# An expert layer's first slot list moved ahead of weight conversions, and output writes that no longer wait for one another

## The chip, the cores and the metric

The kernel runs on one core of a Trainium2 chip. The metric is the device time of one execution in microseconds (us), given as the median over runs. An execution is also recorded by the hardware profiler; the recording's span is a little shorter than the execution's own time.

## The reference, cut to what matters

Four batches of 576 tokens pass through attention (8 heads, window of 128), then through a block that adds the real part of a two-dimensional Fourier transform and an MLP (512 to 2048 to 512), and then through the layer that the change touches: each token goes to one of 8 experts, which it takes from its own logits or from the token before it.

```python
for b in range(B):
    prev_e = -1
    for s in range(S):
        fresh_e = int(np.argmax(logits[b, s]))
        if s == 0 or local_gate[b, s] < 0.5:
            e = fresh_e
        else:
            e = prev_e if prev_e >= 0 else fresh_e
        prev_e = e
        ...
        h = np.maximum(x[b, s] @ w1[e], 0.0)
        out[b, s] = p[e] * (h @ w2[e])
```

x is 2304 x 512, w1[e] is 512 x 1024, w2[e] is 1024 x 512, all float32. An expert works on the tokens that chose it, and each token's row of `out` is written once.

## The kernel before

Each float32 product is made of three TensorE products (`mm3`, L171 to L173: high by high, high by low, low by high). `split` makes the two halves: the high half is a copy on ScalarE (L167, "CAST" in the trace), the low half a subtraction on VectorE (L168, which reads the high half), so every conversion of a piece of weights is one instruction on ACT and then one on DVE.

The experts are ranked by their load. The work after the MLP runs in this order. Expert "-1" is the first ranked expert's first 256 tokens (`early`); then comes r = 0, the same expert with 224 more rows and with the same weights, then r = 1 (384 rows), and so on to r = 7 (216 rows). Each is one pass of `ffn`. It runs over eight blocks of 128 hidden columns, and for each of them PE makes the hidden product `hps` (12 matmuls), ACT the relu `h` or `hE` (L631) and DVE its low half (L634). The second product `acc` of a block stands on PE behind the hidden product of the block after it. It needs the relu for its L171 and the low half for its L173.

Around `ffn` stand two generators that are taken a step at a time.

- `expert_weights(r, e)` loads four chunks c0 to c3 of an expert's weights. Each chunk is a pair of 512 KB loads on SP's queue (L1235 for w1, L1236 for w2) into one of two buffers, and four conversions, two for w1 and two for w2. The next load into a buffer waits until the four conversions that read it are done. In the trace the loads are `we<-in_w`, the converted weights `t`.
- `expert_inputs(r)` loads the slot lists of a rank (`ids`, three loads on SP), adds them on DVE (L1275), turns them into row numbers and scales `idn` (L1277, L1278), gathers the rows of x (`xg`, an indirect DMA that POOL issues, L1250, one for each 128 rows), transposes them on PE (L603, `tps`) and splits them to `xTe`.

`emit` scales a finished `acc` into `yo` on ACT (L1261, or L1257 for a folded tail) and writes it by an indirect DMA that POOL issues (L1262, `out<-yo,idn`). `yo` has two buffers. All writes go to the one tensor `out`, and each waits until the write before it has landed.

While expert -1 runs, the kernel steps through r = 1's weights and r = 0's rows (loop at L1376). Before the change `pre_.step(2)` places two conversions behind each half block, and `beside.step(TE)` takes three steps of `expert_inputs(0)`: list and first gather, second gather, first transposes. A scheduler then puts the recorded instructions into one list for each engine. The engines run their lists in order, so an instruction that waits holds up all that stands behind it on its engine. `issue_after(x)` makes the scheduler place what is recorded inside it behind x, and `behind()` is an `issue_after` on the last hidden product, relu and low half.

Of the kernel before, what the change touches and what calls it, by code (L numbers as in the profile page):

```python
# [26 lines left out]
NT = B * S  # L27
# [132 lines left out]
def build(ctx, tc, a, out):  # L160
# [5 lines left out]
    def split(hi, lo, src, eng=None):  # L166
        nc.scalar.copy(hi, src)  # L167
        return (eng or nc.vector).tensor_tensor(out=lo, in0=src, in1=hi.bitcast(F32), op=ALU.subtract)  # L168
# [445 lines left out]
    def ffn(xT, n, chunks, ps_h, acc, hidden, sums, tail=0):  # L614
# [6 lines left out]
        for f in range(nf + 1):  # L621
# [16 lines left out]
            if f > 0:  # L638
# [3 lines left out]
                for t, c in enumerate(range(0, n, P)):  # L642
                    if g == 0:
                        acc.append(sums[t % len(sums)].tile([P, DM], F32, tag=("acc0", "acc1", "acc2", "g")[t], name="acc"))
                    m = min(P, n - c)
                    if tail and m < P:
                        for j in range(2):
                            nc.tensor.matmul(acc[t][0:step + m], lhsT=h[:, c:c + step + m], rhs=t2[:, j, g % per], start=g == 0 and j == 0, stop=g == nf - 1 and j == 1)  # L648
                        continue
                    mm3(acc[t][0:m], h[:, c:c + m], h[:, low + c:low + c + m], t2[:, 0, g % per], t2[:, 1, g % per], g == 0, g == nf - 1)  # L650
                yield
# [552 lines left out]

    def expert_weights(r, e):

# [6 lines left out]
        if r < 0:  # L1213
# [3 lines left out]
            for i in range(len(loads) + RB - 1):  # L1217
# [9 lines left out]
                for m in (slice(0, n // 2), slice(n // 2, n)):  # L1227
                    split(w[:, 0, m], w[:, 1, m], x[:, m])
                    yield
            return  # L1230
        for c in range(F // CB):
            t1, t2 = chunksE[r][c]
            x = act.tile([P, 2, 4 * CB], F32, tag="xT", name="we")
            x1, x2 = x[:, 0].rearrange("p (k f) -> p k f", k=4), x[:, 1].rearrange("p (k f) -> p k f", k=per)
            nc.sync.dma_start(out=x1.unsqueeze(1), in_=w1[:, bass.ds(e, 1), :, c * CB:(c + 1) * CB])  # L1235
            nc.sync.dma_start(out=x2.unsqueeze(1), in_=w2[:, bass.ds(e, 1), c * per:(c + 1) * per, :])  # L1236
            for i in range(2):
                m = slice(2 * i, 2 * i + 2)
                split(t1[:, 0, m], t1[:, 1, m], x1[:, m])
                yield  # L1240
            for i in range(per):
                split(t2[:, 0, i], t2[:, 1, i], x2[:, i])
                yield
# [8 lines left out]

    def emit(acc, idx, m=P, both=False):
        y = act.tile([P, DM], F32, tag="y", name="yo")
# [5 lines left out]
        else:  # L1260
            nc.scalar.activation(y[0:m], acc[0:m], AF.Copy, scale=idx[0:m, 2:3].bitcast(F32))  # L1261
        nc.gpsimd.indirect_dma_start(out=out, out_offset=IOA(ap=idx[0:m, 1:2], axis=0), in_=y[0:m], in_offset=None,  # L1262
                                     bounds_check=NT - 1, oob_is_err=False)

# [6 lines left out]
    def slot_ids(x, nt, lists):  # L1271
# [5 lines left out]
        nc.vector.tensor_copy(n[:, 0:nt, 0:2], x0[:, :, 0:2])  # L1277
        nc.vector.tensor_copy(n[:, 0:nt, 2:3].bitcast(F32), x0[:, :, 2:3])  # L1278
        return n
# [96 lines left out]
    for n, _ in enumerate(ffn(xTs.pop(-1), EARLY, chunksE[-1], ps_h, acc, hidden, (ps_a, ps_a))):  # L1376
        if xp is None:
            beside.step(2 if n < 4 else 1)
        if xp is None and not beside.q:
            c2.close()  # L1380
            xp = ctx.enter_context(pool("xp", 2, reuse_waits="tile"))
            pre_.add(expert_weights(1, er[1]))
            pre_.step()
            beside.add(expert_inputs(0))
            beside.step(TE)
        elif xp is not None and n < 15:
            pre_.step(2)
    for t, x in enumerate(acc):
        emit(x, ids[-1][:, t])
    beside.drain()  # L1390

# [5 lines left out]
    def single(xT, chunks, idx):  # L1397

        acc = ps_a.tile([P, DM], F32, tag="acc0", name="acc")
        for c in range(0, len(chunks), 2):  # L1400
# [9 lines left out]
            for f in range(4):  # L1410
                t2 = chunks[c + f // per][1]
                mm3(acc, t[:, 0, f, 0:P], t[:, 1, f, 0:P], t2[:, 0, f % per], t2[:, 1, f % per], c + f == 0, c == 2 and f == 3)
        emit(acc, idx)

# [6 lines left out]
    for r in range(E):  # L1421
# [6 lines left out]
        for n, _ in enumerate(ffn(xTs.pop(r), CAPS[r], chunksE[r], ps_h, acc, hiddenE, (ps_a, ps_a, ps_a2, ps_g), tail_of(CAPS[r]))):  # L1428
            pre_.step(1 if r else 2)
            if n >= 2:  # L1430
# [65 lines left out]
```

## Time and profile before

| what | us |
|---|---|
| three runs | 969.30, 969.94, 970.32 (median 969.94) |
| the profiled execution's own time | 969.35 |
| its span in the trace | 967.6 |
| PE busy in the span | 909.6 (94%) |
| DVE / ACT / POOL busy | 513.5 / 379.7 / 241.1 |

The mean granted clock of TensorE over the span is 0.974 of full speed. An engine's busy time counts its instructions from start to end. Rows of the timeline give start, duration, engine, line, operation, result<-sources, and in brackets the idle time of the engine just before with what released it. "SPq" is the queue on which SP issues loads. A row of waits names who waited for whom, the total in us, how many times and the longest. A row of a stretch gives its bounds and length and the busy us (instructions) of PE, PEld, DVE, ACT and POOL, then the granted clock as a share of full speed, the DMA engines' busy share and GB/s.

Expert -1 ends and r = 0 begins between 705 and 725 us of the span. r = 0's products run from 724.5 to 749.9, and the last product ends near 951.

### The profile page before, as it was taken

How to read it: one execution, taken by the hardware profiler on the slowest of the kernel's cores; microseconds unless marked ns; L12 is line 12 of the kernel's file. 1: busy time of each engine (PE TensorE's matmuls, PEld its weight loads, DVE VectorE, ACT ScalarE, POOL GpSimd, SP SyncE). 2: the span in 40 equal slices, each digit the busy share in tenths (PEclk: the TensorE clock that was granted, in tenths of full speed). 3: DMA queues.
4: the chain of work that ended last, by engine and by line, in shares of the span. 5: the costliest groups of instructions: out<-in, count | busy, mean ns of one | idle time of the engine just before them, and what ended most of it. 6: DMA issues, size and time to landing. Idle time of an engine off the chain costs nothing. (4 is left out here: it accounts for less than half of the span.)

```text
span 967.6 us, 16131 instructions
## 1 busy us (share of the span) xinstructions
PE 909.6 (94%) x5889; PEld 751.8 (78%) x5889; DVE 513.5 (53%) x1308; ACT 379.7 (39%) x993; POOL 241.1 (25%) x365
## 2 busy tenths in 40 slices
PE   8988899989999999999999999998979999999993
PEld 4546576776787898899888888887758898888782
DVE  5778756835655467511334435358656446556410
ACT  4674564543553245421111111114245455445310
POOL 2314631330322046210111312123123211122100
PEclk9989999999999999999999999999989999999997
DMA  9913351541312594263554443426167555465100
GB/s 326 368 70 114 132 153 44 159 131 44 117 38 78 168 339 120 66 152 66 110 109 109 109 104 63 102 71 202 52 207 251 171 173 188 160 190 175 66 20 20
DMA packets 109037, 129.15 MB, mean 133 GB/s; under 512 B 16222, under 2 KB 78046, under 8 KB 108884
## 3 DMA queue, kind: packets, MB, share of 16 engines
q1 hardware_dynamic: 83636, 103.95, 33.4%
q0 software_dynamic: 22720, 19.36, 9.4%
q10 hardware_dynamic: 2592, 4.72, 1.3%
q8 instruction: 48, 0.79, 0.4%
q14 instruction: 41, 0.34, 0.1%
HBM read 99.65 MB, written 30.87 MB: 135 GB/s over the span
## 5 line engine op out<-in xcount | busy, mean ns | idle before, releaser
L631 ACT ACTIVATE h<-hps 128x256 fp32r<-128x256 f32 x152 | 58.2, 383 | 270.5 <-PE hps L173 267.2
L634 DVE SCALAR_TENSOR_TENSOR h<-hps,h 128x256 fp32r<-128x256 f32 x152 | 63.7, 419 | 170.0 <-ACT h L631 169.9
L171 PE MATMUL acc<-t,h 128*128 128x512 f32 x304 | 126.9, 417 | 2.1 <-ACT h L631 1.1
L173 PE MATMUL acc<-t,h 128*128 128x512 f32 x304 | 122.2, 402 | 2.2 <-DVE h L634 2.2
L172 PE MATMUL acc<-t,h 128*128 128x512 f32 x304 | 121.8, 401 | 0.3 <-POOL t L168 0.3
L168 DVE TENSOR_TENSOR t<-we,t 128x512 fp32r<-128x512 f32 x128 | 85.7, 705 | 43.2 <-ACT t L167 40.8
L167 ACT CAST t<-we 128x512 fp32r<-128x512 f32 x128 | 73.5, 619 | 38.6 <-PE acc L648 17.4
L171 PE MATMUL hps<-xT,t 128*128 128x256 f32 x288 | 85.5, 297 | 2.5 <-ACT t L167 2.2
L171 PE MATMUL hps<-xTe,t 128*128 128x320 f32 (+7 forms) x288 | 86.3, 300 | 1.1 <-ACT xTe L167 1.1
L173 PE MATMUL hps<-xT,t 128*128 128x256 f32 x288 | 83.1, 289 | 4.2 <-POOL t L168 4.2
L172 PE MATMUL hps<-xTe,t 128*128 128x320 f32 (+7 forms) x288 | 85.8, 298 | 0.0
L173 PE MATMUL hps<-xTe,t 128*128 128x320 f32 (+7 forms) x288 | 85.5, 297 | 0.0
L171 PE MATMUL hps<-xTb,t 128*128 128x256 f32 x288 | 83.2, 289 | 0.0
L172 PE MATMUL hps<-xT,t 128*128 128x256 f32 x288 | 83.1, 289 | 0.0
L172 PE MATMUL hps<-xTb,t 128*128 128x256 f32 x288 | 81.8, 284 | 0.0
L173 PE MATMUL hps<-xTb,t 128*128 128x256 f32 x288 | 81.8, 284 | 0.0
L406 ACT ACTIVATE t<-t,mx 128x128 f32<-128x128 f32 (+1 forms) x160 | 62.5, 393 | 30.5 <-DVE mx L399 26.4
L173 PEld LDWEIGHTS acc<-t,h 128*128 128x128 f32 x304 | 58.2, 192 | 17.3 <-DVE h L634 3.7
L171 PEld LDWEIGHTS acc<-t,h 128*128 128x128 f32 x304 | 57.7, 190 | 15.5 <-issue 4.4
L171 PEld LDWEIGHTS hps<-xT,t 128*128 128x128 f32 x288 | 56.4, 196 | 11.0 <-ACT t L167 3.3
L172 PEld LDWEIGHTS acc<-t,h 128*128 128x128 f32 x304 | 58.1, 191 | 7.9 <-POOL t L168 0.6
L634 DVE SCALAR_TENSOR_TENSOR hE<-hps,hE 128x256 fp32r<-128x256 f32 (+4 forms) x96 | 30.8, 349 | 61.4 <-ACT hE L631 60.4
(285 smaller groups left out, 2027.9 us busy)
## 6 DMA issues: line engine op xcount, KB each, us to landing
we<-in_w SPq DMA_DIRECT2D x64, 512.0 KB
rw<-in_w_ch SPq DMA_DIRECT2D x32, 512.0 KB
qkt<-in_qk SPq DMA_DIRECT2D x15, 642.0 KB
nd<-xT SPq DMA_DIRECT2D x18, 512.0 KB
xTb<-nd POOLq DMA_DIRECT2D x18, 512.0 KB
vt<-in_v SPq DMA_DIRECT2D x16, 384.0 KB
pd<-y ACTq DMA_DIRECT2D x18, 256.0 KB
ub<-ud SPq DMA_DIRECT2D x18, 256.0 KB
```

The source lines that it names most:

```text
L167: nc.scalar.copy(hi, src)
L168: return (eng or nc.vector).tensor_tensor(out=lo, in0=src, in1=hi.bitcast(F32), op=ALU.subtract)
L171: nc.tensor.matmul(o, lhsT=wh, rhs=xh, start=start, stop=False, **kw)
L172: nc.tensor.matmul(o, lhsT=wh, rhs=xl, start=False, stop=False, **kw)
L173: return nc.tensor.matmul(o, lhsT=wl, rhs=xh, start=False, stop=stop, **kw)
L406: nc.scalar.activation(t[0:m, j], t[0:m, j], AF.Exp, bias=mx[0:m, j:j + 1], scale=-1.0, accum_out=sums[0:m, j:j + 1])
L631: last["relu"] = nc.scalar.activation(h[:, 0:n], hps[:, 0:n], AF.Relu)
L634: last["rest"] = nc.vector.scalar_tensor_tensor(out=h[:, lo:lo + c1 - c0], in0=hps[:, c0:c1], scalar=0.0, in1=h[:, c0:c1].bitcast(F32), op ...
```

## The change

Three things change. First, r = 1's DVE conversions of weights are recorded under `issue_after(lists[0])`, where `lists[0]` is the last instruction on r = 0's list (`idn`), and the conversions of expert -1's loop are recorded under `behind()` and spread otherwise: two steps at first, then none until n is over 12. What is left of r = 1's weights (two chunks) is converted in r = 0's pass, one step for each half block and under `behind()`. Second, r = 0's first transposes are recorded behind the acc product that is last at n = 14, and the two writes of expert -1 are recorded behind the last `split`. Third, each write of `out` is declared independent of the write just before it.

```diff
@@ expert_weights
+    def expert_weights(r, e, lists=None):
+        def turn_():
+            return tc.issue_after(lists[0]) if lists else nullcontext()
+
...
+            if lists is not None and c == 0:
+                yield
             for i in range(2):
                 m = slice(2 * i, 2 * i + 2)
-                split(t1[:, 0, m], t1[:, 1, m], x1[:, m])
+                with turn_():
+                    split(t1[:, 0, m], t1[:, 1, m], x1[:, m])
                 yield
...
@@ emit
+        if alone and wrote:
+            tc.declare_no_dep(w.ins, wrote[-1], reason="each token has one slot, so the rows are others")
+        wrote.append(w.ins)
...
@@ loop of expert -1
-            pre_.add(expert_weights(1, er[1]))
+            lists = []
+            soon_ = 2
+            pre_.add(expert_weights(1, er[1], lists))
             pre_.step()
             beside.add(expert_inputs(0))
-            beside.step(TE)
+            beside.step(TM)
+            lists.append(last["idn"].ins)
         elif xp is not None and n < 15:
-            pre_.step(2)
+            with behind():
+                pre_.step(2 if soon_ or n > 12 else 0)
+            soon_ = max(soon_ - 1, 0)
+            if n == 14:
+                with tc.issue_after(last["acc"].ins):
+                    beside.step()
+    beside.drain()
     for t, x in enumerate(acc):
-        emit(x, ids[-1][:, t])
-    beside.drain()
+        with tc.issue_after(last["hi"].ins):
+            emit(x, ids[-1][:, t])
...
@@ loop over r
-            pre_.step(1 if r else 2)
+            with nullcontext() if r else behind():
+                pre_.step()
```

`last["hi"]`, `last["acc"]` and `last["idn"]` are set in `split`, `ffn` and `slot_ids`. Since each write still depends on the write two before it, at most two are under way.

On DVE near the end of expert -1, before: 7716 to 7718 are r = 1's converted weights (c0's w1, c0's w2, c1's w1), 7729 is r = 0's list, 7735 its row numbers, and h_7806 and h_7839 are hidden blocks 5 and 6.

```order
L634 SCALAR_TENSOR_TENSOR h_7806<-hps_7793,h_7806 128x256
L168 TENSOR_TENSOR t1_7716<-we_7724,t1_7716 128x512 x2
L168 TENSOR_TENSOR t2_7717<-we_7724,t2_7717 128x512
L1275 TENSOR_TENSOR ids_7729<-ids_7729 128x8
L168 TENSOR_TENSOR t2_7717<-we_7724,t2_7717 128x512
L1275 TENSOR_TENSOR ids_7729<-ids_7729 128x8
L634 SCALAR_TENSOR_TENSOR h_7839<-hps_7826,h_7839 128x256
L1277 CAST idn_7735<-ids_7729 128x2x2
L1278 COPY idn_7735<-ids_7729 128x2
L168 TENSOR_TENSOR t1_7718<-we_7778,t1_7718 128x512 x2
```

The same place after; the list is 7727, its row numbers 7733, blocks 5 to 7 are h_7790, h_7812 and h_7834.

```order
L634 SCALAR_TENSOR_TENSOR h_7790<-hps_7777,h_7790 128x256
L1287 TENSOR_TENSOR ids_7727<-ids_7727 128x8
L634 SCALAR_TENSOR_TENSOR h_7812<-hps_7799,h_7812 128x256
L1287 TENSOR_TENSOR ids_7727<-ids_7727 128x8
L1289 CAST idn_7733<-ids_7727 128x2x2
L1290 COPY idn_7733<-ids_7727 128x2
L168 TENSOR_TENSOR t1_7716<-we_7724,t1_7716 128x512 x2
L168 TENSOR_TENSOR t2_7717<-we_7724,t2_7717 128x512 x2
L634 SCALAR_TENSOR_TENSOR h_7834<-hps_7821,h_7834 128x256
L168 TENSOR_TENSOR t1_7718<-we_7837,t1_7718 128x512 x2
```

All four of c0's conversions on DVE have moved from ahead of the row numbers to behind them; the low half of block 6 still stands between the list's two additions.

On ACT in r = 0's pass, before: hE_7940 to hE_8067 are the relus of blocks 1 to 5, and 8172 to 8175 are the weights of r = 2 (c0's w1 and w2, c1's w1 and w2, from loads 8180 and 8258).

```order
L631 ACTIVATE hE_7940<-hps_7927 128x224
L167 CAST t1_8172<-we_8180 128x512 x2
L631 ACTIVATE hE_7976<-hps_7963 128x224
L167 CAST t2_8173<-we_8180 128x512 x2
L631 ACTIVATE hE_8002<-hps_7989 128x224
L167 CAST t1_8174<-we_8258 128x512
L167 CAST xTe_7960<-tps_8005 128x4x128
L167 CAST t1_8174<-we_8258 128x512
L167 CAST xTe_7960<-tps_8018 128x4x128
L631 ACTIVATE hE_8038<-hps_8025 128x224
L167 CAST xTe_7960<-tps_8041 128x4x128
L167 CAST t2_8175<-we_8258 128x512 x2
```

The same pass after, from block 3 (hE_7996) through block 4 (hE_8036) to block 5 (hE_8067); 7722 and 7723 are r = 1's last chunk. Ahead of these rows stand c2's four conversions (7720, 7721) between the relus of blocks 0 to 2, and, between the relus of blocks 2 and 3, one of 7721, one of 7722 and both of 8172.

```order
L631 ACTIVATE hE_7996<-hps_7983 128x224
L167 CAST t1_7722<-we_7976 128x512
L167 CAST xTe_7947<-tps_8001 128x4x128
L167 CAST t2_7723<-we_7976 128x512
L167 CAST t2_8173<-we_8180 128x512 x2
L167 CAST xTe_7947<-tps_8016 128x4x128
L631 ACTIVATE hE_8036<-hps_8023 128x224
L167 CAST t2_7723<-we_7976 128x512
L167 CAST xTe_7947<-tps_8041 128x4x128
L167 CAST t1_8174<-we_8258 128x512 x2
L167 CAST t2_8175<-we_8258 128x512 x2
L631 ACTIVATE hE_8067<-hps_8054 128x224
```

Eight conversions of r = 1 have come into this pass, and those of r = 2 stand ahead of a later relu than before: 8172 ahead of block 3's instead of block 2's, 8173 ahead of block 4's instead of block 3's, and all of 8174 and 8175 ahead of block 5's with nothing of PE's between them. DVE's list has the same order. On SP the load 8180 waits for the last conversion of 7721 on DVE, and the load 8258 for the last of 8173.

On PE at the end of expert -1, the difference (the acc products of block 7, and the transposes of r = 0's first 128 rows):

```order
 L171 MATMUL acc<-t_7075,h 128x512
+L603 MATMUL tps<-ident,xg 128x128 x4
 L172 MATMUL acc<-t_7075,h 128x512
+L173 MATMUL acc<-t_7075,h 128x512
 L171 MATMUL acc<-t_7075,h 128x512
-L603 MATMUL tps<-ident,xg 128x128 x4
-L173 MATMUL acc<-t_7075,h 128x512
 L172 MATMUL acc<-t_7075,h 128x512
 L173 MATMUL acc<-t_7075,h 128x512
```

Two products more stand behind the first transposes than before.

## Rows read from the trace of the kernel before

**Rows 1.** PE's waits from 700 us on: total us, times, longest.

```profile
PE tps L603 <- DMA xg<-x2d,idn: 4.4, 2, 3.4
...
PE hps L171 <- ACT xTe L167: 1.1, 1, 1.1
```

**Rows 2.** PE's timeline: r = 0's transposes, its first product, r = 1's first.

```profile
719.11 1.11 PE L603 MATMUL tps<-ident,xg 128*128 128x128 f32 x4 [3.38 <-DMA xg<-x2d,idn]
...
722.54 0.90 PE L603 MATMUL tps<-ident,xg 96*128 96x96 f32 x4 [1.04 <-DMA xg<-x2d,idn]
724.50 0.77 PE L171 MATMUL hps<-xTe,t 128*128 128x224 f32 x2 [1.06 <-ACT xTe L167]
...
749.93 0.34 PE L171 MATMUL hps<-xTe,t 128*128 128x384 f32 x1
```

**Rows 3.** Four stretches: length, busy of each engine, PEclk, DMA share, GB/s.

```profile
718.00:720.00 2.00, 0.90 (x5) 0.90 (x5) 0.00 (x0) 0.00 (x0) 0.00 (x0) 0.67 0.96 312
720.00:724.50 4.50, 2.40 (x10) 1.29 (x8) 3.21 (x6) 4.25 (x9) 1.01 (x1) 0.50 0.70 179
724.50:728.50 4.00, 4.00 (x18) 3.91 (x19) 3.78 (x10) 2.38 (x5) 1.69 (x2) 0.50 0.77 261
730.00:740.00 10.00, 10.00 (x70) 8.78 (x69) 7.21 (x17) 5.84 (x13) 5.01 (x5) 1.00 0.87 311
```

**Rows 4.** DVE's timeline around r = 0's list.

```profile
713.37 0.42 DVE L634 SCALAR_TENSOR_TENSOR h<-hps,h 128x256 fp32r<-128x256 f32 x1
713.70 0.16 DVE L1277 CAST idn<-ids 128x4 uint32<-128x4 f32 x1
...
713.84 1.28 DVE L168 TENSOR_TENSOR t<-we,t 128x512 fp32r<-128x512 f32 x2
```

**Rows 5.** ACT's timeline: c0's last casts, block 6's relu, two later relus.

```profile
711.35 1.14 ACT L167 CAST t<-we 128x512 fp32r<-128x512 f32 x2 [0.53 <-DMA we<-in_w]
712.40 0.38 ACT L631 ACTIVATE h<-hps 128x256 fp32r<-128x256 f32 x1
...
744.60 0.36 ACT L631 ACTIVATE hE<-hps 128x224 fp32r<-128x224 f32 x1 [1.35 <-PE hps L173]
...
747.33 0.36 ACT L631 ACTIVATE hE<-hps 128x224 fp32r<-128x224 f32 x1 [0.19 <-PE hps L173]
```

**Rows 6.** POOL's timeline: r = 0's gathers, and the last two writes.

```profile
714.64 1.35 POOL L1250 DMA_INDIRECT xg<-x2d,idn  x1 [10.45 <-ACT h L631]
716.30 1.18 POOL L1250 DMA_INDIRECT xg<-x2d,idn  x1 [0.30 <-issue]
...
951.80 1.00 POOL L1262 DMA_INDIRECT out<-yo,idn  x1 [17.20 <-ACT yo L1261]
955.92 1.00 POOL L1262 DMA_INDIRECT out<-yo,idn  x1 [3.12 <-DMA out<-yo,idn]
```

**Rows 7.** SP's queue: loads of c2, of r = 2's c0, c1, c3.

```profile
713.40 0.37 SPq L1235 DMA_DIRECT2D we<-in_w  x1
...
724.33 0.37 SPq L1235 DMA_DIRECT2D we<-in_w  x1
...
727.52 0.37 SPq L1235 DMA_DIRECT2D we<-in_w  x1
...
742.51 0.37 SPq L1235 DMA_DIRECT2D we<-in_w  x1
```

**Rows 8.** The DMA engines' GB/s in 40 slices, 740 to 749 us.

```profile
GB/s 373 346 391 391 364 137 18 18 9 9 18 27 18 0 0 27 77 141 273 391 373 364 378 364 396 400 419 410 400 237 9 0 0 0 0 0 0 0 0 0
```

**Rows 9.** The chain that ended last: the last pair of writes.

```profile
951.80 3.26 DMA out<-yo,idn
...
956.19 0.73 POOL out L1262
```

**Rows 10.** An earlier stretch with PE waits, and the longer wait.

```profile
660.50:664.00 3.50, 3.21 (x11) 2.33 (x12) 3.50 (x6) 1.14 (x2) 1.27 (x1) 0.52 0.75 181
...
660.79 0.79 PE L173 MATMUL acc<-t,h 128*128 128x512 f32 x1 [1.77 <-DVE h L634]
```

More of the change, by code (lines that the diff above doesn't have):

```diff
@@ L166, in split @@
     def split(hi, lo, src, eng=None):
-        nc.scalar.copy(hi, src)
+        last["hi"] = nc.scalar.copy(hi, src)
         return (eng or nc.vector).tensor_tensor(out=lo, in0=src, in1=hi.bitcast(F32), op=ALU.subtract)
@@ L649, in ffn @@
                         continue
-                    mm3(acc[t][0:m], h[:, c:c + m], h[:, low + c:low + c + m], t2[:, 0, g % per], t2[:, 1, g % per], g == 0, g == nf - 1)
+                    last["acc"] = mm3(acc[t][0:m], h[:, c:c + m], h[:, low + c:low + c + m], t2[:, 0, g % per], t2[:, 1, g % per], g == 0, g == nf - 1)
                 yield
@@ L1203, in build @@
     chunksE, xTs, ids = {}, {}, {}
-    def expert_weights(r, e):
+    def expert_weights(r, e, lists=None):
         chunksE[r] = []
@@ L1236, in expert_weights @@
             nc.sync.dma_start(out=x2.unsqueeze(1), in_=w2[:, bass.ds(e, 1), c * per:(c + 1) * per, :])
+            if lists is not None and c == 0:
+                yield
             for i in range(2):
                 m = slice(2 * i, 2 * i + 2)
-                split(t1[:, 0, m], t1[:, 1, m], x1[:, m])
+                with turn_():
+                    split(t1[:, 0, m], t1[:, 1, m], x1[:, m])
                 yield
             for i in range(per):
-                split(t2[:, 0, i], t2[:, 1, i], x2[:, i])
+                with turn_():
+                    split(t2[:, 0, i], t2[:, 1, i], x2[:, i])
                 yield
@@ L1251, in gather, with emit @@
         return g
-    def emit(acc, idx, m=P, both=False):
+    wrote = []
+    def emit(acc, idx, m=P, both=False, alone=True):
         y = act.tile([P, DM], F32, tag="y", name="yo")
@@ L1261, in emit @@
             nc.scalar.activation(y[0:m], acc[0:m], AF.Copy, scale=idx[0:m, 2:3].bitcast(F32))
-        nc.gpsimd.indirect_dma_start(out=out, out_offset=IOA(ap=idx[0:m, 1:2], axis=0), in_=y[0:m], in_offset=None,
-                                     bounds_check=NT - 1, oob_is_err=False)
+        w = nc.gpsimd.indirect_dma_start(out=out, out_offset=IOA(ap=idx[0:m, 1:2], axis=0), in_=y[0:m], in_offset=None,
+                                         bounds_check=NT - 1, oob_is_err=False)
+        if alone and wrote:
+            tc.declare_no_dep(w.ins, wrote[-1], reason="each token has one slot, so the rows are others")
+        wrote.append(w.ins)
     def slot_load(s0, nt, lists):
@@ L1277, in slot_ids @@
         nc.vector.tensor_copy(n[:, 0:nt, 0:2], x0[:, :, 0:2])
-        nc.vector.tensor_copy(n[:, 0:nt, 2:3].bitcast(F32), x0[:, :, 2:3])
+        last["idn"] = nc.vector.tensor_copy(n[:, 0:nt, 2:3].bitcast(F32), x0[:, :, 2:3])
         return n
@@ L1412, in single @@
                 mm3(acc, t[:, 0, f, 0:P], t[:, 1, f, 0:P], t2[:, 0, f % per], t2[:, 1, f % per], c + f == 0, c == 2 and f == 3)
-        emit(acc, idx)
+        emit(acc, idx, alone=False)
     nc.vector.tensor_single_scalar(eid[:, 0], eid[:, 0], 3, op=ALU.arith_shift_right)
```

## The prediction

> **What bounds the kernel now.** The views were read in this order: the page, PE's waits by releaser, PE's timeline with its neighbours, the granted clock by stretch, and the chain that ended last. The busy shares say that PE is the engine that sets the time, so the first question is where PE stands still in the part that the change touches. From 700 us on its largest wait by releaser is 4.4 us for r = 0's gathered rows, in two waits, and there is one of 1.1 us for the split rows [rows 1]. The timeline puts these together: PE waits 3.38 us before the first transposes, 1.04 us before the second and 1.06 us before r = 0's first product at 724.50 [rows 2]. PE's clock then falls too. It is 0.67 from 718 to 720 and 0.50, its lower level of 1.2 GHz, from 720 to 728.5, and it is back at 1.00 in the stretch from 730 [rows 3]. From 724.50 on PE is busy without a gap (4.00 of 4.00 and 10.00 of 10.00 us in two stretches [rows 3]) until r = 1 starts at 749.93 [rows 2], so r = 0 lasts 25.43 us. The reader should see two costs here: a gap that ends late, and some 4 us of full work at half speed behind it, which lose about 2.1 us. The second place is the end of the span. The last write on POOL starts at 955.92 after 3.12 us of waiting for the landing of the write before it, which started at 951.80 [rows 6], and the chain that ended last runs through just that landing of 3.26 us [rows 9].
>
> **The end of the span.** The last write is now released by the write before the last pair, which landed long ago, and by its scaled tile, which ACT had made together with the first of the pair. So POOL can issue it as it issues the second of r = 0's gathers behind the first: issue of 1.00 us [rows 6], then 0.30 us, the gap between the two gathers [rows 6]. It starts at 951.80 + 1.00 + 0.30 = 953.10 in place of 955.92, 2.8 us sooner. What follows the last issue is taken as unchanged. Taken: -2.8 us; bounds 0 (if something else ends the program, below) and -3.1 (the whole wait of 3.12). The earlier pairs of writes lie beside PE's work and are taken at nothing. Their cover is the rest of the next expert's pass; without it each would be worth a wait like this one.
>
> **The list earlier.** Before, the low half of block 6 runs on DVE at 713.37 and r = 0's row numbers at 713.70, and the first gather is issued at 714.64 [rows 4, 6], 0.94 us later. The change takes c0's four conversions out of the way (0.64 us each, half of the 1.28 that a pair takes [rows 4]), but the second addition still stands behind block 6's low half, and that waits for block 6's relu, which on ACT stands behind c0's last casts, which waited for their load until 711.35 and so begin the relu at 712.40 [rows 5]. The low half can run at about 712.85, the addition after it, and the row numbers at about 713.3. That is 0.4 us sooner, not the 2.5 us that four conversions suggest. The first gather is issued at about 714.2 and the second at 715.8, by the spacing of 1.66 us [rows 6].
>
> **The gathers alone on the DMA engines.** The larger effect is on the loads. Before, c2's load was issued at 713.40 [rows 7], between the row numbers and the gathers, with c3's pair behind it; the DMA engines were 0.96 busy from 718 to 720 [rows 3], while the second gather, issued at 716.30, let its transposes start only at 722.54 [rows 2, 6], 6.2 us later. Now c2's load waits for c0's conversions, which stand behind the row numbers: 713.4 + 4 x 0.64 = 716.0. The gathers have the engines nearly to themselves. How long such a gather takes alone no row shows directly; the nearest is a lone write by the same kind of DMA, 3.26 us from start to landing [rows 9]. So the rows land at about 717.4 and 719.1, and the bounds are 717.1 and 718.5 (0.3 us quicker) to the old 719.1 and 722.5. Behind the second landing come its transposes, the split on ACT and DVE: before, 724.50 - 722.54 = 1.96 us [rows 2], at half clock and with ACT busy with conversions and writes. I take 1.5 us, since the split now stands ahead of the writes' scaling. r = 0 then starts at 720.6, 3.9 us earlier; bounds 720.0 to 724.0.
>
> Here a page of the Trainium skill bears on the row. The row shows a gather that takes 6.2 us when two pairs of loads are on their way beside it. "DMA: Bandwidth & Descriptors", section "Issuing engines are not separate DMA queues", says that transfers started from different engines' queues run on the same 16 DMA engines and interleave. By that, the gather's gain is the whole of the difference to a lone transfer, as taken above; if SP's loads and POOL's gathers did not share, the gain would be only the 0.4 us of the list, and r = 0 would start at 724.1.
>
> **The conversions that move into r = 0.** Eight conversions of r = 1 (c2 and c3) now run in r = 0's pass: 8 x 0.64 = 5.1 us on DVE and 8 x 0.57 = 4.6 us on ACT (1.14 a pair [rows 5]). ACT and DVE are 0.58 and 0.72 busy between 730 and 740 [rows 3], so as work this is hidden. Not hidden is what it does to the loads, since each load waits for the conversions that empty its buffer, and the conversions of r = 2 stand ahead of relus. PE's cover is known: a block takes 2.73 us (747.33 - 744.60 [rows 5]), and its relu is wanted one such step after its hidden product. A relu that is late by more than about 2.7 us stops PE. The chain, at r = 0's start of 720.6:
> - Block 2's relu comes two blocks after the start, 5.5 us at full clock and 1.3 for the clock (below), at 727.4. Behind it stands c2's last conversion, so that r = 2's c0 is issued at about 729, before at 724.33 [rows 7].
> - A lone pair of loads is done 4.2 us after its issue: that issued at 742.51 [rows 7] ends in the slice at 746.7 [rows 8] (40 slices of 0.225 us). I take 3.6 us until the w1 half can be converted and 5.0 for the w2 half. c0's casts run at 732.6 to 733.7, and block 3's relu behind them at 733.7. It would have come at 730.2 (727.4 + 2.73), is 3.5 us late, and PE waits about 0.8 us.
> - Block 4's relu stands behind a cast of c3, two splits, another cast and both w2 casts of r = 2's c0. PE waits about 1.5 us.
> - r = 2's c1 is issued when c0's last conversion is through DVE, at about 738.5, before at 727.52 [rows 7]. Its w1 half can be converted at 742.1, its w2 half at 743.5. All four casts, 4 x 0.57, stand ahead of block 5's relu, so it comes at 744.7. Without them it would have come at 739.3 (727.4 + 3 x 2.73, the two waits above, and 1.4 of r = 1's transposes), so that it is 5.4 late and PE waits 2.7; if DVE gets to c0's last conversion 2 us later (three splits and r = 2's list stand there), 4.7. I take 3.5.
>
> The sum of the waits is 5.8 us; bounds 2 and 8.
>
> **The clock.** Before, the lower level cost about 2.1 us. Now the waits ahead of r = 0 are shorter, but PE still stands for some 2.5 us before the first transposes. An earlier stretch shows that waits of 1.77 us and less are enough for a fall, to 0.52 over 3.5 us [rows 10]. I take a loss of 1.3 us in r = 0 after the gap, between nothing and 2.1. A wait of 3.5 us inside r = 0 can bring a second fall; by rows 10 it costs 3.5 x 0.48 = 1.7. I take half, 0.9.
>
> "TensorE: Matmul & The Clock Gate", Part 1, says that the low clock is the default and that activity lifts it. The rows agree so far: each low stretch here follows a wait. By it alone the second fall would be certain and the forecast 0.8 us later.
>
> **The sum.** r = 0 without waits takes 25.43 - 2.1 = 23.3 us. From 720.6: 720.6 + 23.3 + 1.3 + 5.8 + 0.9 = 751.9, against 749.93: +2.0. With the end, 2.0 - 2.8 = -0.8 us. The profiled execution's own time is 969.35, so 968.6 beside it; the median of the runs is 969.94, 0.59 higher, and the same sum from there gives 969.1. I forecast the median: 969.1 us. A measurement of this kernel tells about 0.2% (1.94 us) from no change; so the forecast is "within".
>
> **The rivals.**
> - *The waits in r = 0 stay small (faster).* The relus are late by chains of estimates, and each has 2.7 us of cover. If the loads come a microsecond or so sooner at each turn, the waits total 2 us or less and there is no second fall: 720.6 + 23.3 + 1.3 + 1.5 = 746.7, -3.2, with the end -6.0: about 963.9. For it speaks that DMA engines are free after the gathers; against it, that r = 2's loads wait for conversions that wait for relus.
> - *The load chain takes the gain and more (slower).* The same chain at its long end: block 5's relu waits for a load issued at 740 or later, PE stops for over 4 us, the clock falls there in full, and also after the gap. 721.0 + 23.3 + 2.1 + 8 + 2 = 756.4, +6.5, with the end +3.7: about 973.6. It decides from r = 0 lasting over 34 us (the 25.4 of before, plus 3.9 and 2.8 gained, plus 1.9).
> - *The end doesn't move.* After the last issue at 956.19 [rows 9] the span has still 10.7 us to go. If this tail hangs on something else than the last write, the 2.8 us are not gained: about 971.9 with the rest as forecast.
> - *The gathers are no sooner.* If they land as before, only the 0.4 us of the list remain. r = 0 starts at 724.1 and the chain shifts with it: +3.5 on the forecast, about 972.6. The busy DMA engines speak for the loads as the cause, so it has little chance.
>
> **How the numbers follow.** Forecast (968 to 971.8) 0.42; small waits 0.32; the long chain 0.15; the end that doesn't move 0.06; gathers no sooner 0.05. The last two lie at and above the upper bound of "within"; of their 0.11, 0.07 count as slower and 0.04 as within. So faster by over 0.2% is 0.32, within 0.2% 0.46, slower 0.22. The range from 963.5 to 973.2 takes in most of the small waits and about half of the long chain.
>
> **What would show it.** In the changed kernel's trace: r = 0's first `hps` near 720.6 (gathers), with the first transposes at about 717.5; the row numbers at 713.3; waits "PE acc L171 <- ACT hE L631" in r = 0 that add up to some 6 us, with ACT waiting for `we` ahead of block 3's and block 5's relus; r = 1's first product 2 us later than 749.93; and a last issue on POOL 1.30 us after the one before it. The prediction fails if the waits in r = 0 are under 3 us, if r = 0 starts after 723, or if the last issue still waits.

## The result and the profile after

The change made the kernel slower. Its runs have a median of 977.14 us (973.11 to 981.73, 7 runs) beside 969.30 us before (7 runs, among them the three known ahead of the prediction); the ratio is 1.009 with a 95% interval of 1.0069 to 1.011. The profiled execution of after took 976.56 us, with a span of 974.8.

Executions differ by some microseconds before they come to the place of the change: block 6's relu in expert -1 starts at 712.40 in the trace of before [rows 5], at 710.29 in that of after and at 714.76 in that of e2 below, which has the changed kernel's order up to there. So the times below are counted from that relu. From there to the end of the span it is 255.2 us before and 264.5 us after, +9.3, which agrees with the ratio of the runs (+8.7).

PE's timeline after: r = 0's two transposes, its first product, the three long waits inside r = 0, and r = 1's first product.

```profile
715.91 0.66 PE L603 MATMUL tps<-ident,xg 128*128 128x128 f32 x4 [3.30 <-DMA xg<-x2d,idn]
...
720.47 0.62 PE L603 MATMUL tps<-ident,xg 96*128 96x96 f32 x4 [2.75 <-DMA xg<-x2d,idn]
721.66 0.77 PE L171 MATMUL hps<-xTe,t 128*128 128x224 f32 x2 [0.57 <-ACT xTe L167]
...
738.60 0.50 PE L171 MATMUL acc<-t,hE 128*128 128x512 f32 x1 [1.58 <-ACT hE L631]
...
743.78 0.51 PE L173 MATMUL acc<-t,hE 128*128 128x512 f32 x1 [1.15 <-DVE hE L634]
...
749.78 0.80 PE L171 MATMUL acc<-t,hE 128*128 128x512 f32 x1 [3.48 <-ACT hE L631]
...
758.52 0.33 PE L171 MATMUL hps<-xTe,t 128*128 128x384 f32 x1
```

r = 0 started 11.4 us behind the relu, before 12.1 [rows 2, 5]; it then took 36.86 us in place of 25.43 [rows 2]. Where its waits come from stands on ACT: the casts `t<-we` of r = 2's chunks wait for their loads, and the relus `hE` of blocks 3 and 5 stand right behind them. (The first row holds the relus of blocks 6 and 7 of expert -1, which ran one right after the other.)

```profile
710.29 0.65 ACT L631 ACTIVATE h<-hps 128x256 fp32r<-128x256 f32 x2
...
737.15 1.14 ACT L167 CAST t<-we 128x512 fp32r<-128x512 f32 x2 [5.48 <-DMA we<-in_w]
738.20 0.35 ACT L631 ACTIVATE hE<-hps 128x224 fp32r<-128x224 f32 x1
...
746.76 1.14 ACT L167 CAST t<-we 128x512 fp32r<-128x512 f32 x2 [3.92 <-DMA we<-in_w]
748.33 1.14 ACT L167 CAST t<-we 128x512 fp32r<-128x512 f32 x2 [0.44 <-DMA we<-in_w]
749.38 0.35 ACT L631 ACTIVATE hE<-hps 128x224 fp32r<-128x224 f32 x1
```

PE's wait of 1.15 us between the two is for block 4's low half, which stood on DVE behind conversions and r = 2's slot list:

```profile
742.39 0.69 DVE L168 TENSOR_TENSOR t<-we,t 128x512 fp32r<-128x512 f32 x1
...
743.35 0.38 DVE L634 SCALAR_TENSOR_TENSOR hE<-hps,hE 128x224 fp32r<-128x224 f32 x1
```

SP's queue shows when those loads were issued: r = 1's c2 at 714.00, r = 2's c0 at 731.90 and its c1 at 743.21. Before, the last two were issued at 724.33 and 727.52 [rows 7], so c1's load left 17.8 us later against block 6's relu (743.21 - 710.29 beside 727.52 - 712.40).

```profile
714.00 0.37 SPq L1238 DMA_DIRECT2D we<-in_w  x1
...
731.90 0.37 SPq L1238 DMA_DIRECT2D we<-in_w  x1
...
743.21 0.37 SPq L1238 DMA_DIRECT2D we<-in_w  x1
```

The clock by stretch (columns as in [rows 3]): all of r = 0, its start, and the part around the longest wait.

```profile
721.66:758.52 36.86, 30.35 (x156) 24.96 (x157) 19.84 (x42) 17.28 (x36) 7.90 (x8) 0.83 0.59 186
721.66:727.50 5.84, 5.84 (x25) 5.69 (x26) 2.22 (x7) 2.15 (x5) 4.02 (x4) 0.50 0.63 219
...
748.00:754.60 6.60, 4.82 (x16) 3.93 (x17) 3.89 (x8) 2.79 (x6) 0.00 (x0) 0.51 1.04 317
```

PE was idle for 6.5 of the 36.86 us. It worked 5.84 us at half clock at the start and 4.82 us at 0.51 around the wait of 3.48 us, which lose 2.9 and 2.4 us (at least: both low stretches reach a few tenths past the rows shown). Before there was one such stretch, which reached 4.4 us into r = 0 and lost 2.2.

POOL's timeline: r = 0's gathers, and the last two writes.

```profile
712.18 1.35 POOL L1257 DMA_INDIRECT xg<-x2d,idn  x1 [10.43 <-ACT t L167]
713.84 0.94 POOL L1257 DMA_INDIRECT xg<-x2d,idn  x1 [0.30 <-issue]
...
960.94 1.00 POOL L1271 DMA_INDIRECT out<-yo,idn  x1 [19.51 <-ACT yo L1270]
962.25 1.00 POOL L1271 DMA_INDIRECT out<-yo,idn  x1 [0.30 <-issue]
```

The last write is issued 1.31 us behind the one before it, before 4.12 [rows 6].

### The profile page after: what moved, and what is told of

Its sections match the earlier page's. It is cut to its first block, busy times and chain, and to the rows that moved or that the text cites. A ratio compares the mean times of both kernels' runs of the same rounds, so it can differ in the third digit from the quotient of the medians.

```text
span 974.8 us, 16125 instructions
## 1 busy us (share of the span) xinstructions
PE 908.9 (93%) x5886; PEld 750.3 (77%) x5889; DVE 512.4 (53%) x1308; ACT 379.5 (39%) x993; POOL 243.4 (25%) x365
## 4 chain that ended last, share of the span: by engine, by line
PE 66%; DVE 12%; issue 7%; DMA 7%; ACT 3%; POOL 3%; SPq 1%; POOLq 0%; DVEq 0%; ACTq 0%
PE hps L171 9%; PE hps L172 8%; PE hps L173 8%; PE acc L171 8%; PE acc L173 7%; PE acc L172 7%; DMA we<-in_w 3%; PE o L434 3%; PE zps L577 3%; PE s L391 2%; PE tps L603 2%; DVE t L281 2%; ACT t L167 1%; PE acc L648 1%; PE pt L415 1%
## 5 line engine op out<-in xcount | busy, mean ns | idle before, releaser
L167 ACT CAST t<-we 128x512 fp32r<-128x512 f32 x128 | 73.5, 618 | 52.8 <-DMA we<-in_w 27.7
L406 ACT ACTIVATE t<-t,mx 128x128 f32<-128x128 f32 (+1 forms) x160 | 62.5, 393 | 29.7 <-DVE mx L399 25.4
```

Source lines behind the costliest of these rows:

```text
L167: last["hi"] = nc.scalar.copy(hi, src)
L406: nc.scalar.activation(t[0:m, j], t[0:m, j], AF.Exp, bias=mx[0:m, j:j + 1], scale=-1.0, accum_out=sums[0:m, j:j + 1])
```

## The experiments

The kernels are compared in four stretches, worked out from each one's trace: from block 6's relu to r = 0's first product; r = 0 itself, to r = 1's first product; from there to the last issue on POOL; and from that issue to the end of the span. The last columns give the ratio of the runs to runs of before on the same chip, with its interval. The stretches are of one execution each. Most kernels had 12 runs, e2 10, after 7, e11 6, e7 4 and e4 only 2.

| kernel | to r = 0 | r = 0 | r = 1 to last issue | rest | ratio to before (95%) |
|---|---|---|---|---|---|
| before | 12.1 | 25.4 | 206.0 | 11.7 | 1 |
| after | 11.4 | 36.9 | 203.7 | 12.6 | 1.0090 (1.0069 to 1.0110) |
| e1 writes only | 12.0 | 25.5 | 202.8 | 12.6 | 0.9975 (0.9962 to 0.9989) |
| e2 r = 0 steps as before | 11.9 | 28.8 | 203.0 | 12.4 | 0.9998 (0.9980 to 1.0015) |
| e3 r = 2's weights behind | 10.1 | 27.3 | 204.8 | 12.7 | 1.0006 (0.9988 to 1.0025) |
| e4 gathers first | 9.9 | 36.1 | 202.8 | 12.8 | 1.0076 (1.0048 to 1.0104) |
| e5 list first and writes | 11.7 | 29.8 | 203.2 | 12.3 | 1.0012 (0.9996 to 1.0029) |
| e6 e3, idle products | 10.9 | 25.3 | 205.2 | 12.7 | 0.9966 (0.9944 to 0.9987) |
| e7 all but writes | 10.3 | 34.4 | 206.9 | 11.5 | 1.0085 (1.0063 to 1.0107) |
| e8 e6 and gathers first | 8.6 | 26.3 | 206.4 | 12.8 | 0.9981 (0.9961 to 1.0001) |
| e9 e1, idle products | 13.4 | 24.6 | 204.2 | 13.0 | 0.9988 (0.9972 to 1.0003) |
| e10 list alone | 12.2 | 29.3 | 207.6 | 11.6 | 1.0029 (1.0011 to 1.0046) |
| e11 e12, idle products | 10.3 | 25.2 | 201.5 | 12.9 | 0.9921 (0.9897 to 0.9946) |
| e12 r = 2's past r = 0 | 10.2 | 25.2 | 201.4 | 12.9 | 0.9955 (0.9937 to 0.9973) |

Up to r = 0's first product after, e2, e3, e7 and e12 have one and the same order. Their first column, 10.1 to 11.9 us, therefore shows how far executions differ by themselves; differences of that size in it prove nothing.

**The theory and the rivals.** The theory after the result: r = 2's casts stand ahead of r = 0's relus and wait for loads that are issued late, because each load waits for casts that themselves stand behind relus (the load chain). The rivals: the eight moved conversions cost by themselves, the loss comes from r = 0's late start and low clock, or from the writes.

**e1: the writes alone.** The kernel before with this:

```diff
+        if alone and wrote:
+            tc.declare_no_dep(w.ins, wrote[-1], reason="each token has one slot, so the rows are others")
+        wrote.append(w.ins)
```

> The kernel before with one part of the change alone: each write of out no longer depends on the write just before it. If the loss of the whole change comes from r = 0's pass (the load chain), this part alone is a gain at the end of the span: last issue 1.30 us after the one before it in place of 4.12, so 1.9 to 2.8 us faster than before (ratio 0.9971 to 0.9980), r = 0 as before (25.4 us, no waits in it). If two writes under way disturb the gathers or the weight loads, it is slower than before, and r = 1 to r = 7 are longer than before's 206.0 us from r = 1's first product to the last issue less 2.8.

It was 2.4 us faster by the ratio. The last pair of writes in its trace, and then the end of its span at 966.4:

```profile
952.51 1.00 POOL L1264 DMA_INDIRECT out<-yo,idn  x1 [19.50 <-ACT yo L1263]
953.82 1.00 POOL L1264 DMA_INDIRECT out<-yo,idn  x1 [0.31 <-issue]
```

The issue came 2.8 us sooner, and 0.9 us of it went again behind it (12.6 us from the last issue to the end in place of 11.7). The table shows this for every kernel: 11.5 to 11.7 where writes wait for one another (before, e7, e10), 12.3 to 13.0 where they do not. The writes are a gain, and the loss lies elsewhere.

**e2: r = 0's steps as before.** The changed kernel with one line back:

```diff
-            with nullcontext() if r else behind():
-                pre_.step()
+            pre_.step(1 if r else 2)
```

> The changed kernel with the loop of r = 0 as before: two steps of weight conversions for each half block, not placed behind the last hidden product. The eight conversions of r = 1's c2 and c3 still run after expert -1, but at r = 0's start, and r = 2's conversions stand ahead of the relus where they stood before the change. Load chain: the waits ahead of blocks 3, 4 and 5 go, one of 1 to 2.5 us ahead of block 0's relu comes (c3's casts stand ahead of it), r = 0 lasts 25 to 29 us in place of 36.9, time 966 to 971. If the eight conversions themselves are the cost, r = 0 stays over 33 us and the time over 974.

The long waits went and r = 0 fell to 28.8 us, although the eight conversions of r = 1 still run behind expert -1's products. So conversions as work do not make the long waits. What is left in r = 0, 3.4 us over before, is not what was expected: no relu of block 0 is late, but r = 1's transposes wait 2.1 us for their gathers. DVE makes r = 1's row numbers only at 733.71, behind seven conversions that run from 728.30, so the moved conversions still cost something by this way. PE's timeline, and the stretch from this wait's end:

```profile
740.35 0.66 PE L603 MATMUL tps<-ident,xg 128*128 128x128 f32 x4 [2.14 <-DMA xg<-x2d,idn]
...
740.35:745.00 4.65, 4.65 (x33) 4.18 (x34) 2.38 (x4) 2.41 (x5) 1.88 (x2) 1.00 0.83 264
```

**e3: r = 2's conversions into r = 1's pass.** The changed kernel with the same rule for one pass more:

```diff
-            with nullcontext() if r else behind():
+            with nullcontext() if r > 1 else behind():
```

> The changed kernel with one more pass under the same rule: in r = 1's pass, too, conversions are placed behind the last hidden product and relu, so that r = 2's conversions leave r = 0's pass and run in r = 1's. Load chain: no wait over 1 us in r = 0 and no second fall of the clock; r = 0 lasts 26 to 28 us; r = 1 grows by 2 us at most; time 965 to 968, under before. If the eight moved conversions or the low clock at r = 0's start are the cost, r = 0 stays over 33 us and the time over 974.

r = 0 took 27.3 us, with no wait over 0.6 us:

```profile
720.15:747.46 27.31, 26.72 (x157) 23.36 (x158) 11.52 (x28) 10.13 (x22) 7.90 (x8) 0.88 0.58 182
```

This is the second way of taking r = 2's casts from ahead of r = 0's relus, and again the loss goes. The forecast of a time under before failed: the ratio is 1.0006. All of r = 0's first 6.7 us ran at half clock, and r = 1 to the end kept 2.1 us more than e1: PE waits 2.4 us for slot lists on DVE in the later passes, before 0.7.

**e4: the gathers first.** The changed kernel with c2's load held until the second gather has landed:

```diff
+            if lists is not None and c == 2:
+                gate = tc.issue_after(nc.sync.dma_start(out=landed, in_=last["xg"][0:1, 0:16]).ins)
+            with gate:
                 nc.sync.dma_start(out=x1.unsqueeze(1), in_=w1[:, bass.ds(e, 1), :, c * CB:(c + 1) * CB])
...
```

> The changed kernel, with r = 1's c2 load held on SP until r = 0's second gather has landed (a 64-byte transfer that reads the gathered rows stands ahead of it). If the loads beside it make the gather slow, it lands 3.3 to 3.8 us after its issue in place of 6.6 and r = 0 starts about 3 us sooner against expert -1's end; c2 comes 3 us later and the waits in r = 0 grow, so the time stays within 3 us of the changed kernel. If a gather takes 6 us by itself, r = 0's start does not move.

In after the second gather is issued at 713.84 and its transposes start at 720.47, 6.6 us later. In e4 POOL issues it at 715.09:

```profile
715.09 0.95 POOL L1263 DMA_INDIRECT xg<-x2d,idn  x1 [0.30 <-issue]
```

The transfer on SP's queue that waits for its landing starts at 718.38, so the gather takes at most 3.3 us, and c2's load follows it:

```profile
718.38 0.31 SPq L1242 DMA_DIRECT2D landed<-xg  x1
719.00 0.39 SPq L1244 DMA_DIRECT2D we<-in_w  x1
```

So the loads beside it make the gather slow, but not always as slow as in after. With c2's load again 0.16 us behind it, the second gather of e3 takes 5.1 us; over all traces with a load at that place it is 5.1 to 7.2 us. e3, on POOL and then on PE:

```profile
713.56 0.95 POOL L1257 DMA_INDIRECT xg<-x2d,idn  x1 [0.30 <-issue]
...
718.68 0.90 PE L603 MATMUL tps<-ident,xg 96*128 96x96 f32 x4 [0.42 <-DMA xg<-x2d,idn]
```

r = 0 started 1.5 us sooner than in after, half of what was expected (and within what executions of one order differ by): PE still had five products of expert -1 and the second transposes to do after the first rows landed, at half clock. The time stayed that of the changed kernel (two runs), with waits of 7.5 us for relus and low halves in r = 0. One of them, of 2.19 us, and the clock behind it:

```profile
737.29 0.69 PE L171 MATMUL acc<-t,hE 128*128 128x512 f32 x1 [2.19 <-ACT hE L631]
...
737.50:740.80 3.30, 3.30 (x10) 2.31 (x10) 3.30 (x7) 3.30 (x8) 0.00 (x0) 0.50 0.01 2
```

This wait was followed by a fall to 0.50, e2's of 2.14 us by none.

**e5 and e10: the early list without the moved conversions.** e5 undoes both conversion rules of the changed kernel; e10 is the kernel before with the `expert_weights` part of the change (the `turn_()` lines and the `yield` ahead of them) and nothing else.

```diff
-            with behind():
-                pre_.step(2 if soon_ or n > 12 else 0)
-            soon_ = max(soon_ - 1, 0)
+            pre_.step(2)
...
```

> The changed kernel with both conversion rules undone: two steps of conversions behind each half block in expert -1's loop and in r = 0's, neither placed behind the last hidden product. Kept are the list ahead of DVE's conversions, the placed transposes, the splits ahead of the scaled writes, and the writes without waits. r = 2's conversions stand where they stood before. If the loss is the load chain, no relu in r = 0 waits over 1 us except block 0's (c3's casts stand ahead of it, 0 to 2 us), r = 0 starts 1 to 2 us sooner against block 6's relu than before, r = 0 lasts 25 to 28 us, and the time is 965 to 969, at or under that of the writes alone. If the early list or the placed transposes cost something, it is over 970.

> The kernel before with one part of the change alone: DVE's conversions of r = 1's weights placed behind the last instruction on r = 0's list. Conversion steps, transposes, scaled writes and the waits of the writes as before. From e5, which differs by the writes, the transposes' place and the splits ahead of the scaling: r = 0's first product comes 0 to 1 us sooner against block 6's relu than before's 12.1 us, since c2's load still lies beside the second gather; r = 0 is longer than 25.4 by about what is gained, and the time is within 2 us of before (ratio 0.998 to 1.002). If the early list is a gain that the moved conversions took away, it is 3 to 4 us faster.

Both miss on the side of a loss: e5 is no faster than before although it holds e1's gain of 2.4 us, and e10 is 0.3% slower than before. Three views of e10 show where the early start is lost. POOL's timeline, r = 0's gathers:

```profile
711.84 1.36 POOL L1257 DMA_INDIRECT xg<-x2d,idn  x1 [9.11 <-ACT t L167]
713.50 1.45 POOL L1257 DMA_INDIRECT xg<-x2d,idn  x1 [0.30 <-issue]
```

SP's queue, the loads of r = 1's c2 and c3:

```profile
713.66 0.37 SPq L1238 DMA_DIRECT2D we<-in_w  x1
714.23 0.37 SPq L1239 DMA_DIRECT2D we<-in_w  x1
715.96 0.37 SPq L1238 DMA_DIRECT2D we<-in_w  x1
716.53 0.37 SPq L1239 DMA_DIRECT2D we<-in_w  x1
```

PE's timeline, the second transposes:

```profile
720.69 0.90 PE L603 MATMUL tps<-ident,xg 96*128 96x96 f32 x4 [3.80 <-DMA xg<-x2d,idn]
```

Two pairs of weight loads are issued within 3.0 us of the second gather, and its rows reach PE 7.2 us after its issue. In both kernels r = 1's transposes wait inside r = 0 as well (1.5 and 2.3 us), as in e2. That is part of the 4.4 and 3.9 us by which r = 0 is longer than before; no run settles the rest. The placed transposes and the splits ahead of the scaled writes were not run alone; e5 has them and e10 has not, and since e5 beats e10 by 0.17%, less than the 0.25% of the writes, they are worth little either way.

**e6, e8, e9: the clock.** e6 is e3 with idle products in the gap (products whose result nobody reads); e8 adds e4's hold; e9 is e1 with the same idle products.

```diff
             if n == 14:
                 with tc.issue_after(last["acc"].ins):
+                    w = ps_h[0].tile([P, DM], F32, tag="h", name="fill")
+                    for _ in range(13):
+                        last["fill"] = nc.tensor.matmul(w, lhsT=chunksE[-1][0][0][:, 0, 0, 0:P], rhs=chunksE[-1][0][1][:, 0, 0], start=True, stop=True)
+                with tc.issue_after(last["fill"].ins):
                     beside.step()
```

> The kernel of e3 (r = 2's conversions out of r = 0's pass) with 13 idle products of 128x512 (3.0 us at full clock) on PE behind the acc products of block 6, where PE otherwise waits 3.4 us for the first gather. If the low clock at r = 0's start is what takes the early start away, the clock stays at 1.00 or falls for a shorter time, r = 0 lasts 24 to 25 us in place of 27.3, and the time is 2 to 3 us under that of e3. If r = 0's length there comes from its conversions, it stays at 27.

> The kernel of e6 (clock held by idle products, r = 2's conversions out of r = 0) with r = 1's c2 load held until r = 0's second gather has landed, as in e4. If the slow second gather is what is left of the gap, it lands 3.3 to 3.6 us after its issue, the wait of 2.1 us before the second transposes goes, r = 0 starts 1 to 2 us sooner against block 6's relu than in e6 (10.9 us), and the clock hardly falls; the time is 1 to 3 us under e6's if r = 0's first conversions, whose load comes 3 us later, do not hold the relus of blocks 1 and 2; if they do, waits of 1 to 3 us there take the gain.

> The kernel of e1 (before, with the writes alone changed) with the 13 idle products of e6 at the end of expert -1; in its order 3 of them stand ahead of the first transposes and 10 behind. If the low clock costs r = 0 about 2 us before the change too, the low stretch gets shorter, r = 0 lasts 23.5 to 24.5 us in place of 25.5, and the time is 1 to 2 us under e1's. If the idle products only delay the products behind them, it is the same or up to 2 us slower.

In e6 r = 0 fell from 27.3 to 25.3 us and the ratio from 1.0006 to 0.9966, about 4 us. The clock was not held altogether: it fell at 721.9, and 3.4 us of r = 0 ran at 0.50, in e3 6.7. From block 6's relu to the end the two profiled executions differ by only 0.9 us, so most of the 4 us is measured by the runs and not shown in the traces. In e8 the clock did not fall at all and r = 0 started 8.6 us behind the relu, 3.5 us sooner than before. But r = 1's slot list, which SP loads behind c2's held load, reached DVE only at 725.36, ahead of block 0's low half, for which PE then waited 2.1 us; and the time did not fall below e6's. The stretch of r = 0 in e8, from its first product to r = 1's:

```profile
720.59:746.84 26.25, 24.01 (x157) 20.39 (x157) 11.19 (x28) 10.25 (x22) 8.07 (x8) 1.00 0.75 237
```

PE's wait in it:

```profile
726.49 0.50 PE L173 MATMUL acc<-t,hE 128*128 128x512 f32 x1 [2.11 <-DVE hE L634]
```

PE's 24.0 us of work at 1.00 are near the 23.3 that the prediction took for r = 0 without waits. e9 missed: the clock was back before r = 0, which took 24.6 us, but its first product came 1.4 us later than in e1: ten of the idle products stood between the two transposes. What the products saved they cost.

**e11 and e12: r = 2's conversions past r = 0 only.** e12 is the changed kernel with r = 2's conversions placed behind r = 0's last relu, and nothing else; e11 has e6's idle products too.

```diff
-            with nullcontext() if r else behind():
+            with nullcontext() if r > 1 else past() if r else behind():
                 pre_.step()
...
+        if r == 0:
+            last["relu0"], last["rest0"] = last["relu"], last["rest"]
```

`past()` is an `issue_after` on those two.

> The kernel of e6 with r = 2's conversions placed behind r = 0's last relu and low half alone, no longer behind each block of r = 1, so that r = 3's weights are again converted in r = 1's pass. r = 0 as in e6 (25.3 us, no relu waits). The eight casts of r = 2's c0 and c1 now stand ahead of r = 1's block 0, and c2's and c3's, whose loads are issued only behind them, ahead of blocks 1 and 2. If relus behind casts that wait for late loads are the mechanism, r = 1 shows waits of 1 to 2 us each ahead of its blocks 0 to 2 and the time is 0 to 4 us over that of e6; if not, it is 1 to 2 us under it, by the waits of e6 in the later passes.

> The changed kernel with one thing altered: r = 2's conversions are placed behind r = 0's last relu and low half (as in e11, without its idle products). The relu waits and the second fall of the clock in r = 0 go, so r = 0 lasts 26 to 28 us in place of 34 to 37 and the time is 8 to 11 us under the changed kernel's, at 966 to 969 (ratio to before 0.995 to 0.999). Beside e11 it prices the idle products: 2 to 4 us more than e11, all of it as half-speed work in r = 0. If e11's gain did not come from the clock, it is equal to e11 (961.6).

e12 is the clearest test: one ordering rule takes the changed kernel from 1.0090 to 0.9955. PE's timeline of e12, r = 0's first product:

```profile
723.54 0.48 PE L171 MATMUL hps<-xTe,t 128*128 128x224 f32 x2 [0.57 <-ACT xTe L167]
```

The stretch of r = 0 in e12:

```profile
723.54:748.75 25.21, 25.10 (x157) 22.18 (x158) 13.23 (x31) 11.88 (x26) 7.88 (x8) 0.93 0.65 201
```

No product of r = 0 waits behind the first, and the median of 965.73 us is a little under what was expected. e11 has the lowest median of all, 961.55 us (6 runs) and 0.9921 of before. Its expectation failed: r = 1 shows no waits ahead of blocks 0 to 2, since the loads of r = 2's c0 and c1 were issued in r = 0's pass and had landed, and r = 1 to the last issue is, with e12's, the shortest of all (201.5 us). Against e12 its runs are 0.34% faster, but the two intervals overlap, and the two profiled executions are alike in every stretch (3.4 us of r = 0 at 0.50 in both). What the idle products give here is not shown.

**e7: the change without the writes.** `if alone and wrote:` became `if False:`.

> The changed kernel with each write of out waiting for the one before it, as before the change. If the parts add up, it is 2 to 2.8 us slower than the changed kernel (ratio to before 1.010 to 1.013), with the same waits in r = 0 and the last issue some 4.1 us behind the one before it. If the writes without waits had a part in r = 0's loss, it is faster than the changed kernel.

This one settles little, and its forecast failed (1.0085 in 4 runs, forecast 1.010 to 1.013). Behind r = 0 it lost 2.1 us against after (206.9 + 11.5 beside 203.7 + 12.6), as e1 says; but its profiled r = 0 was 2.4 us shorter, and its runs are those of the changed kernel within the intervals. The second fall of the clock lasted 3.4 us there (from 749.8) and 6.8 in after (from 748.1), behind waits of 3.65 and 3.48 us. So r = 0's length varies between executions of one order with the clock, by about as much as the writes are worth.

## Why the prediction was wrong, point by point

The forecast was "within" at 969.1; the rival that came true is the long load chain, to which the text gave 0.15 and 973.6. It came true by its own sign, r = 0 over 34 us, though PE's longest stop was 3.48 us and not over 4. The mechanism stood there with its place; the sum went wrong by two terms, the gathers and the clock.

- **The end of the span: right, then 0.9 us short.** Last issue 1.31 us behind its forerunner, as worked out (1.30). That what follows is unchanged was wrong: it takes 0.9 us more. The last write lands 3.1 us after its issue in e7 and e10, where it is alone, and 3.9 to 4.4 us in e5, e6 and e11, where the one before it is still under way. The gain is 1.9 us in the traces (2.8 - 0.9), 2.4 in e1's runs.
- **The list: right.** The row numbers came 0.4 us sooner against block 6's relu and the first gather as well: 712.18 - 710.29 = 1.89 us, before 714.64 - 712.40 = 2.24 [rows 5, 6].
- **The gathers alone: the step that failed.** The time of a lone gather was sized well (3.26 taken, at most 3.3 in e4). Wrong was that the gathers would be alone. c2's load was issued at 714.00, 0.16 us behind the second gather, just as the sum has it (716.0 for the load and 715.8 for the gather). The text took an issue ahead of the load for data ahead of the load. In after the second gather took 6.6 us, before 6.2 [rows 2, 6]. So r = 0 started 0.7 us sooner and not 3.9: 3.2 us of the sum. (In e2, e3, e7 and e12, with the same order, it started 0.2 to 2.0 us sooner than before.) On before's time axis, 2.1 us later, the first product comes at 723.8, past the 723 that the text named as a sign of failure, and near the 724.1 of its rival "gathers no sooner". Nor was the step to be had for nothing: e4 kept the load away from the gather, the load left 3.8 us later against block 6's relu than in after, and the time stayed. The Trainium skill, "DMA: Bandwidth & Descriptors", section "Issuing engines are not separate DMA queues", bears on exactly this: transfers started from different engines run on the same 16 DMA engines and interleave. The runs agree (5.1 to 7.2 us beside the load, at most 3.3 without), and the prediction had drawn only half of it: a load issued 0.16 us behind the gather interleaves with it as well.
- **The waits in r = 0: right in place, and in size with some luck.** Forecast 0.8, 1.5 and 3.5 us ahead of blocks 3, 4 and 5, 5.8 in all; measured 1.58, 1.15 and 3.48, 6.2 in all. The loads were issued 10.2 and 21.6 us behind r = 0's start, forecast 8.4 and 17.9. Block 5's relu came 27.7 us behind that start, forecast 24.1; the wait is as forecast because PE, at half clock for longer, came to it later too.
- **The clock: mis-sized.** Taken 1.3 + 0.9 = 2.2 us; measured 2.9 + 2.4 = 5.3. The first loss was taken smaller than before's because the waits ahead of r = 0 would be shorter (about 2.5 us); they were 3.30 and 2.75, and the low stretch reached about 6 us into r = 0, in before 4.4. The second fall was taken at half a chance and came in full (0.51 from 748.0 to 754.6). The Trainium skill, "TensorE: Matmul & The Clock Gate", Part 1, says that the low clock is the default and that activity lifts it, which the text read as a certain second fall. The trace of after agrees for the wait of 3.48 us, but the waits of 1.58 and 1.15 us ahead of it brought no fall (1.00 from 737 to 748): each low stretch here follows a wait, but not each wait brings one.
- **The sum.** r = 0 was to take 31.3 us and took 36.9; 0.4 of the difference is waits, at least 3.1 the clock, and for the other 2.1 at most no row names a cause. With the 3.2 us of the start, the 0.9 at the end and 0.5 between r = 1's start and the last issue these make up the difference between the 9.3 us of the result and the -0.8 of the forecast.
- **Chances.** The waits and the second fall hang on one chain, and the one brings on the other; the text priced them apart. It also priced the long chain and "gathers no sooner" (0.05) as rivals that exclude each other, and in after they came together. By the text's own numbers a start at 724.1 and the long chain's 35.4 us give 759.5, +9.6, with the end +6.8: about 976.7, beside the 977.1 measured.

## What to carry to other kernels

An order in which relus stand behind casts, and casts behind loads that wait for earlier casts, is a loop through three queues: place the conversions of work that is two passes ahead behind the last relu of this pass, and the loop is cut (e12: 1.0090 to 0.9955 by one rule). Issuing a transfer 0.16 us ahead of a competitor's did not keep the competitor off the DMA engines; a wait for the landing did (e4, e8), and it moved the competitor and its users back (by 3.8 us in e4). Price waits and clock together where the first brings on the second.

## What the runs showed of the hardware

A gather of 96 rows of 2 KB that takes at most 3.3 us alone (e4, e8) takes 5.1 to 7.2 with weight loads issued 0.16 us behind it (e3, e10). Writes that do not wait for one another are issued 1.3 us apart, but the last of a pair lands 3.9 to 4.4 us behind its issue (e5, e6, e11) in place of 3.1 (e7, e10), and the span behind it is 0.6 to 1.5 us longer. The granted clock fell to 0.50 in r = 0's first microseconds in all kernels but e4, e8 and e9, for 3.3 to 6.7 us of r = 0's work, and with the same wait of 3.4 us ahead of the first transposes the fall began at different places: before r = 0 in e3 (716.6) and 0.7 us behind its first product in e12 (724.3). Waits of about 2.2 us inside r = 0 came out either way: the clock fell behind 2.19 us in e4 and stayed at 1.00 behind 2.14, 2.11 and 2.28 us in e2, e8 and e10.
